# Values loaded row by row, and one weighting request per group that uses both column halves

## The chip, the cores and the metric

One core of a Trainium2 chip runs the kernel. The metric is device time in microseconds (us) of one execution. Engines: TensorE (PE; its weight loads are listed as PEld), VectorE (DVE), ScalarE (ACT), GpSimd (POOL) and SyncE (SP), whose queue issues all transfers (DMA) of this kernel. Matrix products read SBUF and write PSUM, which has 8 banks of 128 partitions x 512 32-bit columns.

## The reference

Eight batches of banded attention, and behind it a gated feed-forward block that mixes tokens:

```python
scores = scale * np.matmul(q, k.transpose(0, 1, 3, 2))      # 8 batches, 8 heads, 576 tokens, 64 wide
mask_plain = (rel >= 0) & (rel < window)                    # window 32: heads 0 to 3
mask_dil = (rel >= 0) & (rel < window * dilation) & (rel % dilation == 0)   # dilation 4: heads 4 to 7
attn = softmax(np.where(masks, scores, -1e9))
x = np.matmul(attn, v)                                      # heads side by side: 512 features a token
h = np.maximum(x @ w_in, 0.0)                               # 512 -> 1024
u, v = (h[..., :512], h[..., 512:])
v_n = (v - mean(v)) / np.sqrt(var(v) + 1e-06)
v_s = np.einsum('ts,bsd->btd', w_spatial, v_n) + b_spatial[None, :, None]
out = (u * v_s) @ w_out                                     # 512 -> 512
```

With a reordering of the dilated heads' tokens on the host, every head is a band: a block of 32 queries sees its own block of 32 keys and the one before.

## The kernel before, in words

**Tiling of the attention.** Heads are handled in pairs (hp, 4 a batch), two pairs make a group G (2 a batch, 16 in all). Within a group i is the pair, j the head in the pair. The 18 blocks of 32 queries are cut into 3 units of 6 blocks (`unit`, L776): the scores of a unit go to two banks (L796, stationary 64 x 32, moving 64 columns, rows 64j, columns 32(2i + j)), then the masks, the softmax (L830 to L861) and a transposition by VectorE (L866) that leaves the weights as `pT`, with the keys of (i, j) on partitions 32(2i + j).

**Values.** `values_in` (L763) loads a group's values into one buffer `kqv` of 11: four transfers, one for each (i, n), with n the block parity; the source is seen as "j k t d" (2 heads, 32 rows, 9 double blocks, 64 elements), the destination as 64 partitions x 9 x 64. A piece without a break is 64 elements of 4 bytes.

**Weighting.** `weighted` (L874) multiplies values by weights: for each half h of the tokens (9 blocks each) it asks for two banks, one per pair i, and for each key block c and each (i, j) issues one product with 32 rows (partitions 32(2i + j)), 64 stationary columns (the values) and 64 or 32 moving columns (the weights of one or two query blocks), L895. Its result goes to bank i, partitions 64j to 64j + 63: row group 2i + j always uses column half j. A half needs only the units that its blocks touch. After each half the weights whose blocks are over are given back, and four evacuations per group, `evacuated` (L918), copy the banks to `raw` on ScalarE (L927: 128 partitions x 288 columns, x64 in all).

**Behind the attention.** `features_in` (L931) splits `raw` into a high and a low part `x`; `v_tile` (L953, products L971 and L991) makes v and normalises it; `upper` (L1044), in the first batch, or `piece` (L1308, products L1279) makes u; `gate` (L1081, products L1091) mixes tokens; `piece` also makes the output in sums of block products, copied from the bank by ScalarE (L1365) or added by VectorE (L1342) and stored from `ur` (L1380). All 32-bit weights are split at the start into high and low parts, on ScalarE, VectorE, GpSimd or PE (`weight`, L565, with products L600 to L602; `spatial`, L633, with L651).

**What sets the order.** Nothing is scheduled by hand line by line. Each function above is a strand that yields what it waits for, the buffers it wants, and the engine with a planned cost. `Timeline.run` (L365) plays all strands against a model of the engines, always takes the one with the smallest planned start plus a share of its rank, and emits its instructions in that order into each engine's queue; on the chip each queue then runs in that order. The ranks are sums of a place in the batch and of numbers in the tables `SHIFT`, `SECOND`, `FIRST` and `RANKS`; `LOADS` (L239) is the order of the first loads on SP. `warm` (L1393) fills PE with products of zeros (L1399) while the planner's clock is under 30 us.

Of the kernel before, what the change touches and what calls it, by code (L numbers as in the profile page):

```python
# [26 lines left out]
    ('differences', 0): 3.431,  # L27
    ('differences', 1): -1.388,
    ('factor', 0): -1.117,
    ('factor', 1): 2.398,  # L30
    ('factor', 10): -3.001,
    ('factor', 11): 10.273,
    ('factor', 12): -3.976,
    ('factor', 13): 5.666,
    ('factor', 14): -7.301,
    ('factor', 2): 4.983,
    ('factor', 3): 0.711,
    ('factor', 4): 4.444,
    ('factor', 5): 2.348,
    ('factor', 6): 2.155,  # L40
    ('factor', 7): 1.428,
    ('factor', 8): 6.612,
    ('factor', 9): -2.995,
    ('features_in', 0): -0.537,
    ('features_in', 1): -0.751,
    ('features_in', 2): -1.809,
    ('features_in', 3): -0.424,
    ('gate', 0): -1.362,
    ('gate', 1): -1.076,
    ('gate', 2): -1.219,  # L50
    ('gate', 3): -2.27,
    ('gate', 4): -0.312,
    ('gate', 5): 0.11,
    ('gate', 6): -3.137,
    ('gate', 7): -0.085,
    ('heads_in', 0): -2.791,
    ('heads_in', 1): -12.584,
    ('heads_in', 2): -10.815,
    ('heads_in', 3): -13.398,
    ('piece', 0): -6.162,  # L60
    ('piece', 1): -3.011,
    ('piece', 10): 0.769,
    ('piece', 11): -5.597,
    ('piece', 12): -14.941,
    ('piece', 13): -3.803,
    ('piece', 14): 0.777,
    ('piece', 15): -2.117,
    ('piece', 16): 0.282,
    ('piece', 17): 1.018,
    ('piece', 18): -1.97,  # L70
    ('piece', 19): -1.676,
    ('piece', 2): -5.321,
    ('piece', 20): 1.502,
    ('piece', 21): 0.917,
    ('piece', 22): -2.788,
    ('piece', 23): 0.713,
    ('piece', 24): 1.033,
    ('piece', 25): -0.444,
    ('piece', 26): 1.61,
    ('piece', 27): 3.92,  # L80
    ('piece', 3): 0.345,
    ('piece', 4): -1.75,
    ('piece', 5): -7.219,
    ('piece', 6): -5.255,
    ('piece', 7): 0.574,
    ('piece', 8): -1.49,
    ('piece', 9): -6.48,
    ('unit', 0): 1.147,
    ('unit', 1): 0.659,
    ('unit', 2): 1.12,  # L90
    ('unit', 3): 1.555,
    ('unit', 4): 1.236,
    ('unit', 5): 0.864,
    ('v_tile', 0): -0.613,
    ('v_tile', 1): -2.171,
    ('v_tile', 2): 0.491,
    ('v_tile', 3): -0.547,
    ('v_tile', 4): 0.875,
    ('values_in', 0): 12.349,
    ('values_in', 1): 2.363,  # L100
    ('weighted', 0): 1.183,
    ('weighted', 1): -2.05,
}
SECOND = {
    ('differences', 0): 6.862,
    ('differences', 1): -4.682,
    ('factor', 0): -2.244,
    ('factor', 1): -7.324,
    ('factor', 10): -20.21,
    ('factor', 11): -11.603,  # L110
    ('factor', 12): -4.699,
    ('factor', 13): -10.917,
    ('factor', 14): 5.579,
    ('factor', 2): -2.131,
    ('factor', 3): -4.247,
    ('factor', 4): -1.839,
    ('factor', 5): 1.75,
    ('factor', 6): -3.017,
    ('factor', 7): 4.928,
    ('factor', 8): 6.82,  # L120
    ('factor', 9): -6.234,
    ('features_in', 0): -0.721,
    ('features_in', 1): 0.97,
    ('features_in', 2): -1.126,
    ('features_in', 3): 1.888,
    ('gate', 0): -4.65,
    ('gate', 1): -7.026,
    ('gate', 2): -9.988,
    ('gate', 3): -3.396,
    ('gate', 4): -7.372,  # L130
    ('gate', 5): -4.948,
    ('gate', 6): -4.213,
    ('gate', 7): -4.797,
    ('heads_in', 0): 2.901,
    ('heads_in', 1): 1.879,
    ('heads_in', 2): -11.28,
    ('heads_in', 3): -7.996,
    ('piece', 0): 6.664,
    ('piece', 1): -1.839,
    ('piece', 10): -3.696,  # L140
    ('piece', 11): -21.918,
    ('piece', 12): -4.586,
    ('piece', 13): 0.226,
    ('piece', 14): -13.768,
    ('piece', 15): -3.663,
    ('piece', 16): -5.818,
    ('piece', 17): -3.092,
    ('piece', 18): -3.654,
    ('piece', 19): 2.989,
    ('piece', 2): -6.168,  # L150
    ('piece', 20): -3.531,
    ('piece', 21): -29.215,
    ('piece', 22): -4.653,
    ('piece', 23): -2.368,
    ('piece', 24): -4.298,
    ('piece', 25): -7.047,
    ('piece', 26): 1.593,
    ('piece', 27): -8.907,
    ('piece', 3): -10.342,
    ('piece', 4): -9.305,  # L160
    ('piece', 5): 10.496,
    ('piece', 6): 3.592,
    ('piece', 7): 1.672,
    ('piece', 8): 2.058,
    ('piece', 9): -6.368,
    ('unit', 0): -4.01,
    ('unit', 1): -2.025,
    ('unit', 2): -3.272,
    ('unit', 3): -6.272,
    ('unit', 4): -8.821,  # L170
    ('unit', 5): -2.784,
    ('v_tile', 0): -5.232,
    ('v_tile', 1): -3.657,
    ('v_tile', 2): -2.764,
    ('v_tile', 3): -2.977,
    ('v_tile', 4): -3.818,
    ('values_in', 0): -10.326,
    ('values_in', 1): -3.974,
    ('weighted', 0): 1.018,
    ('weighted', 1): -10.872,  # L180
}
FIRST = {
    ('differences', 0): -17.708,
    ('factor', 0): -10.773,
    ('factor', 1): -8.285,
    ('factor', 10): -6.201,
    ('factor', 2): 9.259,
    ('factor', 3): -0.6,
    ('factor', 4): -12.498,
    ('factor', 5): -7.58,  # L190
    ('factor', 6): 5.807,
    ('factor', 7): -4.97,
    ('factor', 8): -9.831,
    ('factor', 9): -10.954,
    ('features_in', 0): -1.8,
    ('features_in', 1): -3.03,
    ('features_in', 2): 2.51,
    ('features_in', 3): 7.399,
    ('gate', 0): 6.142,
    ('gate', 1): 10.462,  # L200
    ('gate', 2): 2.373,
    ('gate', 3): -1.83,
    ('gate', 4): 1.615,
    ('gate', 5): 1.296,
    ('gate', 6): 1.467,
    ('gate', 7): 3.736,
    ('piece', 0): 0.034,
    ('piece', 1): -2.549,
    ('piece', 10): 0.916,
    ('piece', 11): -0.114,  # L210
    ('piece', 12): -6.838,
    ('piece', 13): 4.458,
    ('piece', 2): -2.984,
    ('piece', 3): 4.445,
    ('piece', 4): -18.587,
    ('piece', 5): -8.75,
    ('piece', 6): -2.472,
    ('piece', 7): -5.156,
    ('piece', 8): -0.366,
    ('piece', 9): -0.029,  # L220
    ('unit', 0): -16.896,
    ('unit', 1): -3.357,
    ('unit', 2): -3.181,
    ('unit', 3): -3.174,
    ('unit', 4): -3.978,
    ('unit', 5): -2.628,
    ('upper', 0): -2.081,
    ('upper', 1): -10.204,
    ('upper', 2): -0.74,
    ('upper', 3): 0.052,  # L230
    ('v_tile', 0): -2.1,
    ('v_tile', 1): -6.845,
    ('v_tile', 2): -1.186,
    ('v_tile', 3): -5.317,
# [172 lines left out]
def tile_banded_attention_gated_moe(  # L407
# [22 lines left out]
    nc = tc.nc  # L430

    B, NPAIR, _, S = kT.shape
# [1149 lines left out]
```

## Time and profile before

| | |
|---|---|
| time, median of 3 runs | 601.1 us (600.82 to 604.26) |
| the profiled execution's own time | 601.41 us |
| its span, first to last instruction | 599.6 us |
| busy | PE 540.0, DVE 381.1, ACT 334.3, POOL 191.8 us |
[...]

The span is cut into stretches below. [...] A busy time can only be read beside the waits: an engine that is idle while another is the bound costs nothing.

### The profile page before, as it was taken

Reading aid. Unit: us, or ns where it says so; the run is one execution under the profiler, and the core shown is the slowest. Engines: PE = TensorE matmul, PEld = TensorE weight load, DVE = VectorE, ACT = ScalarE, POOL = GpSimd, SP = SyncE. Lnnn points to the kernel's source line nnn. Section 1 sums busy time; section 2 is a strip of 40 time slices with the busy share of each in tenths; the row PEclk is TensorE's granted clock in tenths of the full one; section 3 lists DMA queues with packets and bytes.
Section 4 is the critical chain, followed back from the end, with each engine's and each line's share of the span. In section 5 each row is a group of like instructions: output and inputs, shape, how many; then the busy total and the mean of one; then the engine's idle time right before and its main releaser. Section 6 shows DMA issues by size and latency. Waiting matters only on the chain.

```text
span 599.6 us, 18457 instructions
## 1 busy us (share of the span) xinstructions
PE 540.0 (90%) x7828; PEld 492.3 (82%) x7828; DVE 381.1 (64%) x878; ACT 334.3 (56%) x938; POOL 191.8 (32%) x226
## 2 busy tenths in 40 slices
PE   9803898689989996999999999999998999999997
PEld 6603676689889975988999889898998899899997
DVE  6611687659995483766686567745784578647545
ACT  5711679454775453664576367454874478447414
POOL 4300015413841442222441264225431363226100
PEclk9965899879999997999999999999999999999999
DMA  8322713133242212222014221232114302100102
GB/s 295 126 67 77 256 35 109 40 108 97 52 139 59 58 45 86 59 57 88 21 47 113 56 89 59 78 97 90 52 37 133 102 21 59 45 1 21 61 2 79
DMA packets 58535, 46.71 MB, mean 78 GB/s; under 512 B 39378, under 2 KB 48594, under 8 KB 58452
## 3 DMA queue, kind: packets, MB, share of 16 engines
q1 hardware_dynamic: 58452, 45.53, 25.4%
q8 instruction: 61, 1.00, 0.7%
q14 instruction: 22, 0.18, 0.1%
HBM read 36.08 MB, written 9.44 MB: 76 GB/s over the span
## 4 chain that ended last, share of the span: by engine, by line
PE 72%; DMA 9%; DVE 8%; SPq 4%; issue 3%; ACT 2%; POOL 1%; DVEq 0%; ACTq 0%; POOLq 0%
PE bank L1279 26%; PE bank L1091 15%; PE bank L971 12%; PE bank L895 6%; PE bank L796 5%; DMA kqv<-in_vw_dram 4%; DMA out_dram<-ur 3%; SPq L771 2%; DMA kqv<-in_qT_dram 2%; PE bank L991 2%; PE bank L1399 2%; PE bank L1071 1%; PE bank L1070 1%; DVE fac L537 1%; PE bank L600 1%
## 5 line engine op out<-in xcount | busy, mean ns | idle before, releaser
L1091 PE MATMUL bank<-wt,fac 128*128 128x288 f32 x768 | 115.7, 300 | 0.8 <-ACT ur L1365 0.8
L1091 PEld LDWEIGHTS bank<-wt,fac 128*128 128x128 f32 x768 | 106.9, 190 | 2.8 <-ACT ur L1365 1.3
L971 PE MATMUL bank<-wih,x 128*128 128x512 f32 x256 | 84.6, 397 | 0.0
L895 PE MATMUL bank<-pT,kqv 32*64 32x64 f32 (+1 forms) x2688 | 49.2, 226 | 38.4 <-DMA kqv<-in_vw_dram 30.4
L1365 ACT COPY ur<-bank 128x288 f32<-128x288 f32 x120 | 47.0, 397 | 59.5 <-PE bank L1279 33.6
L895 PEld LDWEIGHTS bank<-pT,kqv 32*64 32x64 f32 x2688 | 46.3, 140 | 39.8 <-DMA kqv<-in_vw_dram 31.5
L838 ACT ACTIVATE p<-p,nm 128x64 f32<-128x64 f32 x180 | 60.4, 342 | 10.7 <-DVE nm L832 10.7
L861 POOL TENSOR_TENSOR p<-p,rv 128x384 f32<-128x384 f32 x48 | 41.0, 855 | 71.1 <-DVE rv L859 71.1
L1016 POOL TENSOR_TENSOR rs<-rs,halfneg 128x1 f32<-128x1 f32 (+1 forms) x40 | 30.4, 761 | 100.1 <-DVE rs L1013 99.5
L1279 PE MATMUL bank<-fac,woh 128*128 128x288 f32 x256 | 55.0, 305 | 6.9 <-ACT ur L1365 5.8
L971 PEld LDWEIGHTS bank<-wih,x 128*128 128x128 f32 x256 | 49.4, 193 | 10.2
L537 DVE TENSOR_TENSOR x<-raw,x 128x576 fp32r<-128x576 f32 x32 | 29.8, 933 | 38.2 <-ACT x L942 38.2
L927 ACT COPY raw<-bank 128x288 f32<-128x288 f32 x64 | 30.5, 561 | 41.8 <-PE bank L895 41.4
L1342 DVE TENSOR_TENSOR ur<-ur,bank 128x288 f32<-128x288 f32 x90 | 39.3, 448 | 20.5 <-PE bank L1279 14.8
L1208 ACT CAST fac<-ur 128x576 fp32r<-128x576 f32 x56 | 36.8, 670 | 26.1 <-DVE ur L1077 22.4
L971 PE MATMUL bank<-wil,x 128*128 128x512 f32 x128 | 50.8, 397 | 0.0
L537 DVE TENSOR_TENSOR fac<-ur,fac 128x576 fp32r<-128x576 f32 x56 | 42.4, 779 | 12.6 <-ACT fac L1208 12.4
L1265 POOL TENSOR_TENSOR ur<-ur,ur 128x576 f32<-128x576 f32 x28 | 41.4, 1481 | 26.9 <-DVE fac L537 19.7
L1279 PEld LDWEIGHTS bank<-fac,woh 128*128 128x128 f32 x256 | 42.4, 193 | 9.2 <-ACT ur L1365 6.3
L866 DVE STREAM_TRANSPOSE pT<-p 128x384 f32<-128x384 f32 x48 | 27.2, 571 | 33.7 <-PE bank L895 25.0
L796 PE MATMUL bank<-kqv 64*32 64x64 f32 x2304 | 41.4, 219 | 6.6 <-issue 3.4
L1265 POOL TENSOR_TENSOR raw<-raw,raw 128x576 f32<-128x576 f32 x21 | 30.2, 1437 | 50.8 <-DVE fac L537 26.7
(157 smaller groups left out, 1159.9 us busy)
## 6 DMA issues: line engine op xcount, KB each, us to landing
kqv<-in_vw_dram SPq DMA_DIRECT2D x64, 144.0 KB
out_dram<-ur SPq DMA_DIRECT2D x64, 144.0 KB
kqv<-in_kT_dram SPq DMA_DIRECT2D x30, 288.0 KB
kqv<-in_qT_dram SPq DMA_DIRECT2D x30, 288.0 KB
kqv<-in_w_in_dram SPq DMA_DIRECT2D x8, 512.0 KB
kqv<-in_w_out_dram SPq DMA_DIRECT2D x4, 512.0 KB
kqv<-in_w_spT_dram SPq DMA_DIRECT2D x5, 288.0 KB
kqv<-in_kT_dram SPq DMA_DIRECT2D x2, 192.0 KB
```

The costliest lines, as they stand in the source:

```text
L537: nc.vector.tensor_sub(out, a, b.bitcast(F32))
L796: nc.tensor.matmul(s[w][q * QB : q * QB + QB, e, :], kq[r, :S].rearrange("p (u n i t) -> p u t n i", n=2, i=QB, t=US)[:, (u + places[b, pa ...
L838: nc.scalar.activation(p[:, e, j], s[j][:, e] if first else p[:, e, j], AF.Exp, bias=nm[:, i : i + 1], scale=SCALE if first else 1.0, accu ...
L861: nc.gpsimd.tensor_mul(flat, flat, spread_out(rv))
L895: nc.tensor.matmul(acc[i][1][1][j * D : j * D + D, o : o + len(run) * QB], v[r, c * D : c * D + D], probs[b, G, u][1][r, at : at + len(run ...
L971: nc.tensor.matmul(pm, x[a][:, cols], wi[w][:, c, NF:], start=c == 0 and n == 0, stop=c == NC - 1 and n == 2)
L1091: nc.tensor.matmul(pv, left[:, a, i, m * P : m * P + P], wt[:, k, h, w, i], start=n == 0, stop=False, skip_group_check=True)
L1208: nc.scalar.copy(dst[:, 0], src)
L1265: (eng.tensor_add if kind == "s" and n == 1 else eng.tensor_sub)(at(to), at(left), at(right))
L1279: nc.tensor.matmul(bank[:, :HS], lhs, rhs, start=fresh and n == 0, stop=n == 5, skip_group_check=not fresh or kind == "s")
L1342: nc.vector.tensor_add(ob[1][:, m], ob[1][:, m], bank[:, :HS])
L1365: nc.scalar.copy(ob[1][:, m], bank[:, :HS])
```

## The change

Four things change, and the tables of ranks and the order of loads with them.

- `values_in` issues eight transfers per group in place of four, one for each (i, n, j), each with 32 rows outermost in source and destination; the planned cost goes from 2.6 + 1.5 to 4.2 + 2.0.
- `weighted` asks once per group: for all three units' weights and the values, four banks and `raw`. Its products are the same 84 per group, in an order in which one key block's products of token half 0 and of token half 1 take turns; those of half 1 write column half 1 - j in place of j. Weights and values are given back at the end. The planned cost is 1.35 in place of 0.8 twice.
- `evacuated` waits for the whole group; for token half 1 it copies twice 64 partitions, crosswise, in place of once 128.
- planned costs of `unit` (0.6 to 0.68, the first group's 0.72 to 0.77) and of the transposition (0.47 to 0.5) change, which emit the same instructions.

```diff
 SHIFT = {
-    ('differences', 0): 3.431,
+    ('differences', 0): 0.468,
...
 LOADS = """
-wi00 wi10 kq1a kq0a kq1b kq0b kq3 sp0 kq2 sp3 wi12 sp1 bias wo2 wi11 v1 wi01 v0 sp2 wi02 wo0 wi03 wo3 wi13 wo1
-sp4
+sp4 kq1b wi00 wi12 kq0a kq0b kq1a kq2 wi11 kq3 wi10 wo0 v0 v1 sp3 wi03 wi02 sp2 sp1 wi13 wi01 wo3 wo1 sp0 wo2
+bias
 """.split()
...
-        (big,) = yield DMA, 2.6, 1.5
+        (big,) = yield DMA, 4.2, 2.0
         for i, n in itertools.product(range(2), range(2)):
             src = vw[b, 2 * G + i, (n + 1) * QB : (n + 2) * QB].rearrange("k (t j d) -> j k t d", j=2, d=D)
-            dst = big[1][:, :BIG].rearrange("p (t n d) -> p t n d", n=2, d=D)
-            nc.sync.dma_start(dst[i * 2 * QB : (i + 1) * 2 * QB, :, n, :], src)
+            for j in range(2):
+                to = (2 * i + j) * QB
+                nc.sync.dma_start(big[1][to : to + QB, :BIG].rearrange("p (t n d) -> p t n d", n=2, d=D)[:, :, n, :], src[j])
...
+        yield [("pT", b, G, u) for u in range(NU)] + [("values", b, G)]
+        yield "av bank av bank av bank av bank raw"
+        got = yield PE, 1.35, 0.0
+        acc = [[got[4 * h + 2 * i : 4 * h + 2 * i + 2] for i in range(2)] for h in range(2)]
...
+        runs = []
         for h in range(2):
+            for c in range(h * HB - h, h * HB + HB):
+                to = [g for g in (c, c + 1) if h * HB <= g < h * HB + HB]
+                split = len({g // (2 * US) for g in to}) > 1
+                runs += [(len([r for r in runs if r[1] == h]) + n, h, c, run) for n, run in enumerate([[g] for g in to] if split else [to])]
+        for n, h, c, run in sorted(runs):
...
+            for i, j in itertools.product(range(2), range(2)):
                 r = slice((2 * i + j) * QB, (2 * i + j + 1) * QB)
+                col = (j ^ h) * D
+                nc.tensor.matmul(
+                    acc[h][i][1][1][col : col + D, o : o + len(run) * QB],
...
-        yield ACT, 0.465 if hp >= NPAIR // 2 else 0.3, 0.1
-        nc.scalar.copy(dst, acc[1][1][:, :HS].rearrange("p (r j) -> p r j", r=2))
+        src = acc[1][1][:, :HS].rearrange("p (r j) -> p r j", r=2)
+        for n in range(1 + h):
+            yield ACT, 0.465 if hp >= NPAIR // 2 else 0.3, 0.1
+            to, at = (slice(n * D, n * D + D), slice(D - n * D, 2 * D - n * D)) if h else (slice(0, P), slice(0, P))
+            nc.scalar.copy(dst[to], src[at])
```

## Rows read from the trace of the kernel before

**Rows 1.** Busy time by stretch; after PEclk the DMA share and GB/s.

```profile
0.00:27.00 27.00, 24.18 (x371) 18.42 (x372) 17.60 (x55) 16.99 (x62) 10.61 (x24) 1.00 0.68 230
27.00:55.00 28.00, 3.90 (x29) 2.67 (x31) 3.87 (x10) 3.18 (x9) 2.23 (x3) 0.64 0.27 72
55.00:66.00 11.00, 10.13 (x335) 8.86 (x336) 6.88 (x14) 7.78 (x16) 0.00 (x0) 0.82 0.61 206
66.00:130.00 64.00, 53.54 (x821) 44.28 (x820) 40.88 (x97) 39.83 (x113) 19.76 (x24) 0.89 0.32 94
130.00:250.00 120.00, 110.58 (x1453) 100.85 (x1449) 86.44 (x198) 68.68 (x191) 48.88 (x53) 0.97 0.25 71
250.00:566.00 316.00, 307.36 (x4627) 287.35 (x4619) 207.90 (x476) 188.29 (x530) 110.31 (x124) 1.00 0.22 64
```

**Rows 2.** Who waited for whom: PE to 66, 66 to 130, 200 to 320; ACT.

```profile
PE bank L895 <- DMA kqv<-in_vw_dram: 24.1, 3, 12.1
...
PE bank L895 <- DMA kqv<-in_vw_dram: 6.3, 2, 4.6
...
PE bank L1279 <- ACT ur L1365: 5.8, 1, 5.8
...
ACT ur L1365 <- DMA out_dram<-ur: 6.4, 1, 6.4
```

**Rows 3.** SP's queue: issues by line (ns least/median/most), then in order of time.

```profile
L771 SPq DMA_DIRECT2D kqv<-in_vw_dram x64: 537/3980/7048, 14.2 to 505.0; - x64
...
L753 SPq DMA_DIRECT2D kqv<-in_kT_dram x34: 328/432/4118, 1.6 to 473.3; - x34
...
14.22 15.85 SPq L771 DMA_DIRECT2D kqv<-in_vw_dram  x4
...
34.20 13.92 SPq L771 DMA_DIRECT2D kqv<-in_vw_dram  x4
...
217.96 4.15 SPq L771 DMA_DIRECT2D kqv<-in_vw_dram  x1
...
226.82 18.92 SPq L1380 DMA_DIRECT2D out_dram<-ur  x6
```

**Rows 4.** Busy time of a stretch in which values alone are loaded, columns as before.

```profile
500.00:508.00 8.00, 8.00 (x145) 7.70 (x145) 7.14 (x18) 5.86 (x18) 2.49 (x3) 1.00 0.16 37
```

**Rows 5.** Issues by size (queries as keys; the spatial blocks are 288 KB too).

```profile
kqv<-in_kT_dram SPq DMA_DIRECT2D x30, 288.0 KB
...
kqv<-in_w_in_dram SPq DMA_DIRECT2D x8, 512.0 KB
```

**Rows 6.** The weighting on PE: a group in order of time; a stretch, L895 alone.

```profile
384.04 2.75 PE L895 MATMUL bank<-pT,kqv 32*64 32x64 f32 x168
...
54.85:59.10 4.25, 4.25 (x156) 4.24 (x156) 0.53 0.17 67
```

**Rows 7.** The scores on PE in order of time.

```profile
95.55 0.89 PE L796 MATMUL bank<-kqv 64*32 64x64 f32 x48
...
106.67 1.56 PE L796 MATMUL bank<-kqv 64*32 64x64 f32 x96
```

**Rows 8.** From the chain: a 32-bit product of 288 columns, two instructions.

```profile
79.58 0.48 PE bank L651 x2
```

**Rows 9.** A stop inside the weighting; instructions of PE; the instruction queue.

```profile
262.88 0.42 PE L895 MATMUL bank<-pT,kqv 32*64 32x64 f32 x11 [0.94 <-issue]
...
PE 540.0 (90%) x7828; PEld 492.3 (82%) x7828; DVE 381.1 (64%) x878; ACT 334.3 (56%) x938; POOL 191.8 (32%) x226
...
q8 instruction: 61, 1.00, 0.7%
```

**Rows 10.** ScalarE's copies by line: 1 partition, 128 partitions, and the evacuation.

```profile
L713 ACT CAST wb<-kqv x2: 667/667/667, 17.7 to 18.4; 1x576 fp32r<-1x576 f32 x2
...
L657 ACT CAST wa<-kqv x1: 677/677/677, 76.7 to 76.7; 128x576 fp32r<-128x576 f32 x1
...
L927 ACT COPY raw<-bank 128x288 f32<-128x288 f32 x64 | 30.5, 561 | 41.8 <-PE bank L895 41.4
```

More of the change, by code (lines that the diff above doesn't have):

```diff
@@ new lines @@
+    ('piece', 27): 2.135,
+    ('piece', 3): -2.111,
+    ('piece', 4): -2.378,
+    ('piece', 5): 1.404,
+    ('piece', 6): -1.667,
+    ('piece', 7): -0.342,
+    ('piece', 8): -2.98,
+    ('piece', 9): -6.786,
+    ('unit', 0): 0.628,
+    ('unit', 1): 0.566,
+    ('unit', 2): 1.826,
+    ('unit', 3): 0.588,
+    ('unit', 4): 0.52,
+    ('unit', 5): 0.142,
+    ('v_tile', 0): -0.502,
+    ('v_tile', 1): 0.902,
+    ('v_tile', 2): -0.127,
+    ('v_tile', 3): -1.002,
+    ('v_tile', 4): -0.803,
@@ new lines @@
+    ('piece', 20): -11.571,
+    ('piece', 21): -1.952,
+    ('piece', 22): -17.589,
+    ('piece', 23): -4.77,
+    ('piece', 24): -8.189,
+    ('piece', 25): -13.354,
+    ('piece', 26): -12.138,
+    ('piece', 27): -7.139,
+    ('piece', 3): -3.759,
+    ('piece', 4): 2.184,
+    ('piece', 5): -10.825,
+    ('piece', 6): -2.88,
+    ('piece', 7): 0.609,
+    ('piece', 8): 2.008,
+    ('piece', 9): 1.439,
+    ('unit', 0): -2.064,
+    ('unit', 1): -1.584,
+    ('unit', 2): -2.985,
+    ('unit', 3): 1.179,
@@ new lines @@
+    ('factor', 6): -2.949,
+    ('factor', 7): -1.43,
+    ('factor', 8): -1.637,
+    ('factor', 9): 1.108,
+    ('features_in', 0): 2.028,
+    ('features_in', 1): -0.853,
+    ('features_in', 2): -4.587,
+    ('features_in', 3): 2.266,
+    ('gate', 0): -3.573,
+    ('gate', 1): -2.15,
+    ('gate', 2): -1.355,
+    ('gate', 3): -12.755,
+    ('gate', 4): 1.063,
+    ('gate', 5): -0.7,
+    ('gate', 6): -6.356,
+    ('gate', 7): 5.24,
+    ('piece', 0): -3.587,
+    ('piece', 1): 0.61,
+    ('piece', 10): 1.419,
@@ new lines @@
+    ('piece', 11): -4.959,
+    ('piece', 12): -7.293,
+    ('piece', 13): 5.036,
+    ('piece', 2): -5.483,
+    ('piece', 3): -0.264,
+    ('piece', 4): 0.068,
+    ('piece', 5): -0.742,
+    ('piece', 6): -6.641,
+    ('piece', 7): -15.959,
+    ('piece', 8): 1.594,
+    ('piece', 9): 1.925,
+    ('unit', 0): -5.725,
+    ('unit', 1): -4.044,
+    ('unit', 2): -5.345,
+    ('unit', 3): -0.772,
+    ('unit', 4): -2.004,
+    ('unit', 5): 0.239,
+    ('upper', 0): -9.059,
+    ('upper', 1): 0.37,
@@ L913, in tile_banded_attention_gated_moe @@
+        tl.done("weighted", b, G)
+        for u in range(NU):
+            tl.give(probs[b, G, u])
+        tl.give(values[b, G])
+        for h, i in itertools.product(range(2), range(2)):
+            products[b, 2 * G + i, h] = acc[h][i]
     raws = {}
```

436 lines of the change are left out of this document (169 added, 267 removed).

## The prediction

> **What bounds the kernel now.** I read the busy times by stage first [rows 1]. From 250 to 566 us TensorE (PE) is busy 307.4 of 316 us at the full clock: there it is the bound, and only work taken off PE shortens that stretch. The start is different. From 27 to 55 us PE is busy 3.9 of 28 us, VectorE 3.9 and ScalarE 3.2: nobody works. From 66 to 130 PE is busy 53.5 of 64 at a mean clock of 0.89, from 130 to 250 it is busy 110.6 of 120. The waits of PE say why [rows 2]: 24.1 us until 66 and 6.3 us until 130 are the weighting (L895) waiting for transfers of values; 5.8 us between 200 and 320 is a product waiting for ScalarE's copy L1365, which itself waited 6.4 us for an output transfer to free its buffer. The queue of SyncE (SP) shows why those are late [rows 3]. The four transfers of one group's values hold SP for 15.85 and 13.92 us (median 3.98 us each over all 64), where the median transfer of keys holds it 0.43 us. The second set starts at 34.20, after the first and a weight block stuck behind it, and the weighting that wants it runs from 54.85 [rows 6]. At 217.96 the last of such a set is again in the way: the keys behind it go at 222, the output transfers only at 226.82. While values alone move, 0.16 of the 16 transfer engines are busy and 37 GB/s flow [rows 4], that is two engines or a little more; the first 27 us of the kernel moved 230 GB/s at 0.68 [rows 1].
>
> **Values with rows outermost.** Before, a transfer's source had the two heads as its outermost dimension, 2; after, eight transfers per group have 32 rows outermost on both sides. If a transfer is dealt out by its outermost dimension, 2 explains the two engines, and 32 lets all 16 work: 16/2 x 37 = 296 GB/s, so a group's 590 KB (4 x 144 KB) take 2.0 us. On SP 8 issues cost 8 x 0.43 = 3.4 us, or 8 x 0.54 = 4.3 by the shortest issue of a values transfer [rows 3], in place of some 14 to 16 us. Bounds: at best the waits vanish; at worst it is 8 x 2 us with the same two engines, as now. [...] Here 34 transfers of keys hold SP 0.43 us each in the median, so whatever a transfer costs beyond that overlaps with the next [rows 3].
>
> What that is worth, by stage. The idle stretch: the first weighting starts at 54.85; all it needs except values is there by 27. In the new order of loads two groups' values (1.2 MB) stand behind five weight blocks of 512 KB, one of 288 and four pairs of keys and queries of 576 KB [rows 5], 5.3 MB; 6.5 MB at 230 GB/s [rows 1] is 28 us, the first group's 26. The weighting starts near 28: **27 us** off (bounds 0, if another wait stands there, and 28). What is late next is the rest of the weights: the loads bring 10.5 MB by 66 us (27 x 230, 28 x 72, 11 x 206 [rows 1]), which at 230 GB/s is 46 us; that is the bound of the second rival. Second batch: 6.3 us of waits go, and PE comes out of them at half clock; I take **8 us** (bounds 0 and 10.5, all of PE's idle time from 66 to 130). The output transfer behind values: **5 us** of 5.8 (bounds 0 and 9.4, all idle time from 130 to 250).
>
> **The weighting.** A group is 84 products of 32 bits, which PE runs as 168 instructions in 2.75 us at full clock [rows 6]. With four (row group, column half) tiles each row group uses one half of the columns. [...] A second row says that two tiles in the same rows and different columns do run together: the scores (L796) have four tiles, two in each half of the rows, and 96 take 1.56, 48 take 0.89, so (1.56 - 0.89)/48 = 14 ns each [rows 7]. An instruction of a 32-bit product streams 288 columns in 0.48/2 = 0.24 us [rows 8], so 64 in 53 ns: over four tiles 13.3. Had tiles in the same rows shut each other out it would be 27. So in the change, where the halves of tokens h = 0 and 1 take turns on opposite columns, eight tiles run: the part that streams, 2.75 - (0.89 - 0.67) = 2.53, halves to 1.27, with 0.22 of entry 1.49 us: 1.26 off per group. The ends: 0 (weight loads of one row group may share a path, which no row shows), 1.38 (half of all), and below nothing the drain of the third rival; I take 1.26, as the row of the scores is the nearest.
>
> Part of it comes back. In the middle of dense small products PE stops for 0.9 to 1.0 us with nothing to wait for, three times, of which one row stands here [rows 9]. An instruction queue brings 1.00 MB in 61 packets, and PE has 2 x 7828 instructions, about 257 to a packet [rows 9]; so I take it that a stop comes when a packet's worth is eaten faster than the next arrives. Twice as fast means longer stops and more of them: I charge 0.3 us a group. Net 0.96 x 16 = **15 us**.
>
> One request in place of two: it wants four banks at once, but before both halves already ran without a break (168 in one piece), so nothing new is held. It waits for all three units' transposed weights where h = 0 waited for two; those of a batch are ready long before in the steady stretch. Behind it on PE the next products would wait; I cost this at nothing, covered by the products between scores and weighting, and at 1 us a group if the cover is gone. `evacuated` for h = 0 starts when the group is done: 1.49 us after its start, some 0.1 us later than now (half of 2.75).
>
> **Evacuation.** For h = 1 two copies of 64 partitions: 32 more on ScalarE. A copy with 1 partition costs 667 ns, one with 128 costs 677 [rows 10], so half the partitions save nothing: at the copy's mean of 0.56 [rows 10] 32 are 18 us of ScalarE, 2.2 a batch, where it is busy 188 of 316 us. Hidden, except in the first batch, where features wait for it: **+1 us** (bounds 0 and 4 x 0.56 in each of two batches, 4.5).
>
> **New plan.** The ranks only reorder. With PE busy 307.4 of 316 it can bring at most 8.6 us there; if it left PE as loose as from 130 to 250 (92%) it would cost 16. I take 0. Moved loads: the last spatial block goes from last to first on SP, the bias rows from the thirteenth place to the end, the values from sixteenth and eighteenth to thirteenth and fourteenth; each load still holds SP some 0.43 us for the same bytes.
>
> **Sum.** The profiled execution took 601.4 us (span 599.6 and 1.8 around it; the runs' median is 601.1). 601.4 - 27 - 8 - 5 - 15 + 1 = **547.4 us**.
>
> **Rivals.**
> 1. *Eight tiles are no faster than four*, because weight loads of one row group share a path, or because 15 to 16 ns is what an instruction costs. For: 64 and 32 columns wide products together take 2.53 us, where streaming alone (28 x 53 + 14 x 27 ns per tile) is 1.87. [...] Then 547.4 + 15 = 562.4. [...]
> 2. *The start is bound by the other loads.* 10.5 MB at 206 to 230 GB/s need 46 to 51 us and were in by 66: the last weight comes 15 to 20 us sooner, and if all waits for it and half a group's work is lost besides, 35 us of gain shrink to 12. 547.4 + 23 = 570.4. Against: the products after the first weighting need one load at a time, and from 55 to 66 PE was busy 10.1 of 11 while loads still came.
> 3. *Slower: changing the column half drains the array.* Each group alternates 20 times between h = 0 and 1; at the 0.22 us of a burst's entry (0.89 - 0.67 [rows 7]) that is 4.4 us a group, 70 in all: 562.4 + 70 = 632.4. It decides from 39/(16 x 20) = 0.12 us a change, where the 39 us of the other parts are gone. Against: the scores alternate column tiles at every product, in 14 ns.
> 4. *Transfers don't spread*: two engines as before. Then only the weighting and the copies count: 601.4 - 15 + 1 = 587.4.
>
> **How the numbers follow.** Forecast 0.60, rival 1 0.17, rival 2 0.14, rival 4 0.05, rival 3 0.04. The likeliest's own range is 532 to 560. The range asked for reaches down by PE's other idle time (8.6 from 250 to 566, 4.4 of the 9.4 before) and up past rivals 1 and 2: 528 to 575, leaving out 3 and 4 and a tail. About 1% is what a measurement of this kernel tells from no change. All cases but rival 3 are faster by over 2%; I keep 0.04 for a mixture near nothing: faster 0.92, same 0.04, slower 0.04.
>
> **What would show it.** SP's issues of values near 0.4 to 0.5 us each, eight per group, and a far higher GB/s while they move; no long wait of PE for values; the first weighting before 32 us; 168 weighting products in 1.4 to 1.6 us (2.7 says rival 1) with stops of about 1 to 2 us in more groups; 96 copies at L927's successor, 32 of them on 64 partitions at no less than 0.38 us; batches about 2 us shorter. I am wrong if a values issue still takes 2 us or more, if PE idles over 10 us in one piece after 10 us, or if batches don't shorten.

## The result and the profile after

The median is 550.2 us after (548.4 to 551.9, four runs) against 602.5 before on the same chip: ratio 0.913, interval 0.909 to 0.918. The profiled execution took 551.9 us, span 550.2. Times of runs below are medians; that of shift152 leaves out the longest of its six runs, which lies over 1.5% above its kernel's fastest. The forecast was 547.4 in a range of 528 to 575. So the total came out, and the question for the runs is whether its terms did.

Busy time by stretch, of after (columns as in [rows 1]: from:to and length in us; busy us of PE, PEld, DVE, ACT and POOL, with the number of instructions in brackets; the granted clock of PE as a share of its full clock; the busy share of the core's 16 transfer engines; the GB/s that they moved):

```profile
0.00:27.00 27.00, 25.65 (x474) 19.14 (x474) 19.81 (x58) 15.73 (x58) 9.67 (x23) 1.00 0.80 235
27.00:55.00 28.00, 24.69 (x306) 17.63 (x307) 15.01 (x31) 21.91 (x47) 3.13 (x4) 0.94 0.67 226
55.00:66.00 11.00, 11.00 (x179) 8.06 (x178) 10.52 (x28) 10.62 (x30) 1.62 (x5) 1.00 0.56 159
66.00:130.00 64.00, 58.61 (x979) 52.33 (x977) 57.23 (x133) 44.45 (x133) 36.70 (x40) 0.99 0.25 67
130.00:250.00 120.00, 117.01 (x1840) 108.11 (x1841) 84.92 (x195) 81.21 (x228) 44.44 (x51) 0.98 0.31 86
250.00:520.00 270.00, 264.53 (x3870) 247.18 (x3870) 183.34 (x410) 177.42 (x460) 98.68 (x107) 0.99 0.21 61
```

The dead stretch of 27 to 55 us is gone: PE is busy 24.7 of 28 us where it was 3.9 [rows 1], and the transfers run on at 226 GB/s where they fell to 72. SP's queue says by what. Its issues of values by line (ns least/median/most):

```profile
L772 SPq DMA_DIRECT2D kqv<-in_vw_dram x128: 560/608/1777, 11.5 to 419.1; - x128
```

and in order of time, two groups in one go and the next one:

```profile
11.45 16.07 SPq L772 DMA_DIRECT2D kqv<-in_vw_dram  x16
53.09 5.52 SPq L772 DMA_DIRECT2D kqv<-in_vw_dram  x8
```

A transfer of half the size holds SP for 608 ns in the median instead of 3980, so a group costs SP 5.5 to 8 us instead of some 14 to 16 [rows 3]. Who waits for whom, PE, of after:

```profile
PE bank L897 <- issue: 7.2, 4, 2.1
PE bank L1281 <- ACT ur L1367: 6.0, 1, 6.0
PE bank L1281 <- ACT raw L929: 1.5, 1, 1.5
PE bank L1093 <- ACT x L944: 1.1, 1, 1.1
```

No wait for values is left (30.4 us in [rows 2]). Two kinds stay. One is stops at L897, the weighting, in which PE waits for nothing the profile shows ("issue"). The 1.5 us put down to the copy L929 and the 1.1 us put down to the cast L944 are counted with them: they stand at the same count of instructions, and PE goes on as long after the landing of a packet of its instruction queue as at the others (experiment 5). The copy had ended 0.4 us before; the cast ends just as PE goes on, so that it had a part isn't excluded. The other kind is one wait of 6.0 us for ScalarE's copy L1367. It has the look of the 5.8 us in [rows 2], but isn't the same: there ScalarE waited for an output transfer, here nothing waits for a transfer; the copy is the end of a chain (ScalarE's waits there are 2.2 us for GpSimd's L1267 and 1.9 for VectorE's L537).

The weighting in order of time, first a group with no stop, then one with a stop; and from the page the lines of its copies and its products:

```profile
282.53 2.02 PE L897 MATMUL bank<-pT,kqv 32*64 32x64 f32 x168
...
458.10 2.03 PE L897 MATMUL bank<-pT,kqv 32*64 32x64 f32 x167
...
461.91 0.18 PE L897 MATMUL bank<-pT,kqv 32*64 32x32 f32 x1 [1.78 <-issue]
```

```profile
L929 ACT COPY raw<-bank 64x288 f32<-64x288 f32 (+1 forms) x96 | 49.7, 541 | 16.0 <-PE bank L897 14.7
...
L897 PE MATMUL bank<-pT,kqv 32*64 32x64 f32 (+1 forms) x2688 | 34.8, 229 | 8.0 <-issue 7.2
```

168 instructions take 2.02 us where [rows 6] has 2.75: 0.73 us off a group, not the 1.26 forecast. That is the best case: of the twelve groups that run in one piece five take 2.02 and the others 2.1 to 2.5 us, for a reason that no run shows. In the second group 167 of them run, PE stops for 1.78 us, and the last one follows. The copies behave as forecast: 96, mean 541 ns, the half ones hardly cheaper (538 ns against 548; [rows 10]: 561).

### The profile page after: what moved, and what is told of

Its sections match the earlier page's. It is cut to its first block, busy times and chain, and to the rows that moved or that the text cites. A ratio compares the mean times of both kernels' runs of the same rounds, so it can differ in the third digit from the quotient of the medians.

```text
span 550.2 us, 18561 instructions
## 1 busy us (share of the span) xinstructions
PE 527.7 (96%) x7836; PEld 478.2 (87%) x7836; DVE 385.4 (70%) x878; ACT 360.1 (65%) x970; POOL 194.2 (35%) x226
## 4 chain that ended last, share of the span: by engine, by line
PE 76%; DVE 9%; ACT 6%; DMA 5%; issue 2%; SPq 1%; POOL 0%; DVEq 0%; ACTq 0%
PE bank L1281 31%; PE bank L1093 16%; PE bank L973 12%; PE bank L897 6%; PE bank L797 4%; PE bank L993 2%; DMA kqv<-in_w_in_dram 2%; DMA kqv<-in_w_out_dram 2%; ACT raw L929 2%; PE bank L1073 1%; PE bank L1072 1%; SPq L772 1%; DMA kqv<-in_kT_dram 1%; PE bank L1060 1%; DVE x L537 1%
## 5 line engine op out<-in xcount | busy, mean ns | idle before, releaser
L862 POOL TENSOR_TENSOR p<-p,rv 128x384 f32<-128x384 f32 x48 | 42.6, 888 | 123.6 <-DVE rv L860 122.0
L839 ACT ACTIVATE p<-p,nm 128x64 f32<-128x64 f32 x180 | 60.4, 337 | 10.9 <-DVE nm L833 10.8
L1367 ACT COPY ur<-bank 128x288 f32<-128x288 f32 x120 | 45.7, 397 | 32.4 <-PE bank L1281 28.9
L929 ACT COPY raw<-bank 64x288 f32<-64x288 f32 (+1 forms) x96 | 49.7, 541 | 16.0 <-PE bank L897 14.7
L537 DVE TENSOR_TENSOR fac<-ur,fac 128x576 fp32r<-128x576 f32 x56 | 47.3, 859 | 10.2 <-ACT fac L1210 10.2
L1281 PE MATMUL bank<-fac,woh 128*128 128x288 f32 x256 | 54.1, 302 | 0.0
L1018 POOL TENSOR_TENSOR rs<-rs,halfneg 128x1 f32<-128x1 f32 (+1 forms) x40 | 28.4, 710 | 68.5 <-DVE rs L1015 68.2
L1267 POOL TENSOR_TENSOR raw<-raw,raw 128x576 f32<-128x576 f32 x21 | 33.8, 1608 | 51.6 <-DVE fac L537 40.1
L1210 ACT CAST fac<-ur 128x576 fp32r<-128x576 f32 x56 | 36.7, 673 | 22.9 <-POOL ur L1267 12.5
L1281 PE MATMUL bank<-fac,o 128*128 128x288 f32 x288 | 44.7, 302 | 6.2 <-ACT ur L1367 6.0
L1344 DVE TENSOR_TENSOR ur<-ur,bank 128x288 f32<-128x288 f32 x90 | 39.2, 448 | 14.6 <-PE bank L1281 10.0
L1281 PEld LDWEIGHTS bank<-fac,o 128*128 128x128 f32 x288 | 41.3, 194 | 7.3 <-ACT ur L1367 6.5
L1267 POOL TENSOR_TENSOR ur<-ur,ur 128x576 f32<-128x576 f32 x28 | 41.3, 1475 | 11.8 <-DVE fac L537 8.1
L1281 PEld LDWEIGHTS bank<-fac,woh 128*128 128x128 f32 x256 | 42.8, 193 | 1.9
L897 PE MATMUL bank<-pT,kqv 32*64 32x64 f32 (+1 forms) x2688 | 34.8, 229 | 8.0 <-issue 7.2
L797 PEld LDWEIGHTS bank<-kqv 64*32 64x32 f32 x2304 | 34.8, 119 | 7.3 <-issue 5.9
L897 PEld LDWEIGHTS bank<-pT,kqv 32*64 32x64 f32 x2688 | 32.1, 130 | 10.2 <-issue 8.9
```

Of the source, the lines that this page charges most:

```text
L537: nc.vector.tensor_sub(out, a, b.bitcast(F32))
L797: nc.tensor.matmul(s[w][q * QB : q * QB + QB, e, :], kq[r, :S].rearrange("p (u n i t) -> p u t n i", n=2, i=QB, t=US)[:, (u + places[b, pa ...
L839: nc.scalar.activation(p[:, e, j], s[j][:, e] if first else p[:, e, j], AF.Exp, bias=nm[:, i : i + 1], scale=SCALE if first else 1.0, accu ...
L862: nc.gpsimd.tensor_mul(flat, flat, spread_out(rv))
L897: nc.tensor.matmul(acc[h][i][1][1][col : col + D, o : o + len(run) * QB], v[r, c * D : c * D + D], probs[b, G, u][1][r, at : at + len(run) ...
L929: nc.scalar.copy(dst[to], src[at])
```

## The experiments

Twelve kernels. All ratios are against the kernel before, run beside them on the same chip.

**1. The transfers alone (rows_only), and the rest alone (no_rows).** The first is the kernel before with this edit and nothing else, the second the changed kernel with it undone:

```diff
-            dst = big[1][:, :BIG].rearrange("p (t n d) -> p t n d", n=2, d=D)
-            nc.sync.dma_start(dst[i * 2 * QB : (i + 1) * 2 * QB, :, n, :], src)
+            for j in range(2):
+                to = (2 * i + j) * QB
+                nc.sync.dma_start(big[1][to : to + QB, :BIG].rearrange("p (t n d) -> p t n d", n=2, d=D)[:, :, n, :], src[j])
```

> The kernel before, plan and order kept, with its four transfers of a group's values replaced by the eight with 32 rows outermost. If the transfers' shape is what gave the larger part (theory): about 602.5 - 40 = 562 us, SP's issue of a group's values 5 to 6 us in place of 13 to 16, no wait of TensorE for values over 2 us. If the gain needs the new plan, whose planned costs fit the faster transfers (rival): 585 us or more, with new waits in the place of the old.

> The kernel after, plan and order kept, with the four transfers of before. Theory: the 40 us come back, about 590 us, waits for values of 20 us or more in the first 130 us. Rival (the new order of loads alone, values ahead of weights, would have done it): 565 us or less.

rows_only: 551.3 us, ratio 0.916 (0.912 to 0.920). The eight transfers alone bring 51.5 us, all of the change's gain within the error, where the forecast gave them 40. no_rows: 576.6 us, ratio 0.958 (0.954 to 0.961). Taking them out of the changed kernel costs 26.4 us, only half as much. Matched product by product, no_rows falls 23 us behind the changed kernel in the first 60 us, about as far as the kernel before falls behind rows_only there, and 6.6 more between 160 and 200 us; at the other places where the kernel before loses time (below) it loses none. What in the new order of work spares them was not taken apart. Busy time of two stretches and one wait, of rows_only:

```profile
27.00:55.00 28.00, 23.93 (x398) 18.33 (x397) 18.85 (x39) 18.65 (x41) 1.78 (x2) 0.94 0.62 193
...
66.00:130.00 64.00, 62.28 (x1029) 55.60 (x1026) 56.05 (x135) 46.61 (x149) 36.25 (x38) 1.00 0.33 79
```

```profile
PE bank L896 <- DMA kqv<-in_vw_dram: 1.4, 2, 1.2
```

and of no_rows, the first stretch, PE's longest waits and ScalarE's for transfers:

```profile
27.00:55.00 28.00, 11.64 (x190) 9.04 (x190) 4.32 (x11) 5.38 (x21) 3.43 (x4) 0.65 0.29 80
```

```profile
PE bank L601 <- ACT woh L624: 9.7, 1, 9.7
PE bank L896 <- DMA kqv<-in_vw_dram: 8.7, 2, 5.2
...
ACT kqv L585 <- DMA kqv<-in_w_in_dram: 21.4, 5, 13.8
...
ACT ur L1366 <- DMA out_dram<-ur: 5.1, 1, 5.1
```

SP's queue in no_rows, in order of time:

```profile
12.55 33.40 SPq L771 DMA_DIRECT2D kqv<-in_vw_dram  x8
46.06 3.91 SPq L630 DMA_DIRECT2D kqv<-in_w_spT_dram  x1
50.08 0.84 SPq L562 DMA_DIRECT2D kqv<-in_w_in_dram  x2
```

Eight old transfers hold SP for 33.4 us, and the blocks of weights behind them go out after 46 us. ScalarE waits 13.8 us for one of those (L585), and PE 9.7 us for the copy L624 that ScalarE makes behind it. The old transfers hold up the loads, whoever stands behind them; the 5.1 us, which end at 163 us, are for an output transfer behind values.

Laid on the trace of before by the count of each line's products, rows_only is ahead by 23.7 us at 59 us, 36.2 at 127, 44.8 at 265 and 51.2 at 528. So the first stretch gave 24 (forecast 27), the second batch 12.5 (8), what follows to 265 us 8.6 (5), and the rest 6.4 (0).

Two things make up the excess. One is the clock: up to PE's last product the trace of before has 44.4 us at half clock (0.50), that of rows_only 3.4. PE is busy in 19.0 us of the one and all of the other, and half of the difference, 7.8 us, I count as lost work: an estimate from the products of L1281 in the changed kernel, of which 12 in a row take 3.25 us at a granted clock of 0.50 (from 131.58 us) and 1.75 at 1.00 (from 139.08). Nearly all of it lies in or behind the three places where PE had waited: 35 to 59 us, 117 to 127 and 229.5 to 236. The other is that output transfers stood behind values in four more batches. Of the kernel before, ScalarE's waits for them from 250 to 566 us, PE's waits from 265 to 528 us, and one of the four places in order of time:

```profile
ACT ur L1365 <- DMA out_dram<-ur: 18.9, 4, 5.0
...
PE bank L895 <- issue: 4.2, 4, 1.4
PE bank L796 <- issue: 1.9, 2, 1.0
PE bank L1091 <- ACT ur L1365: 0.8, 2, 0.4
...
333.42 0.58 DVE L866 STREAM_TRANSPOSE pT<-p 128x384 f32<-128x384 f32 x1 [1.38 <-POOL p L861]
...
334.10 2.11 PE L895 MATMUL bank<-pT,kqv 32*64 32x64 f32 x119 [1.45 <-issue]
```

After its wait ScalarE makes the exponentials late, so VectorE transposes the weights late, and PE begins the weighting 0.1 us after the transposition ends, at all four places; the profile names no releaser there, but these are waits and not the stops of experiment 5, whose count of instructions they don't share. rows_only has neither ScalarE's waits nor these of PE; its two stops in the same work come to 2.0 us, where before has 1.9 (L796). Its lead grows at just these places, by 2.3 us at 334, 1.0 at 397 and 2.4 at 460. Added up, rows_only waits 29.0 us less for values, 6.6 less for the copies L1365 and 2.5 less for queries, none of the 4.2 us for late weights, and loses 7.8 less to the clock: 50.1 of the 51.5 us.

**2. Where the weighting's gain comes from (two_copies, h_outer).** In two_copies both token halves use the same column half; the copies stay 96. In h_outer the opposite halves stay, but the first token half is done before the second begins:

```diff
 two_copies
-                col = (j ^ h) * D
+                col = j * D
...
-            to, at = (slice(n * D, n * D + D), slice(D - n * D, 2 * D - n * D)) if h else (slice(0, P), slice(0, P))
+            to, at = (slice(n * D, n * D + D), slice(n * D, n * D + D)) if h else (slice(0, P), slice(0, P))
 h_outer
-        for n, h, c, run in sorted(runs):
+        for n, h, c, run in sorted(runs, key=lambda x: (x[1], x[0])):
```

> The kernel after with token half 1 in the same column half as token half 0 (four tiles in place of eight); the two copies of 64 partitions stay, straight in place of crosswise, every instruction at its place. Theory: the stream of a group's 168 instructions goes back from 1.80 to about 2.53 us, 16 x 0.73 = 12 us, less some 3 us of shorter stops for instructions: 558 to 562 us. Rival (TensorE's time for the weighting is hidden by other waits): 551 us or less, with 2.5 us a group all the same.

> The kernel after with all products of token half 0 before those of half 1, opposite column halves kept: the turns alone are undone. Theory (TensorE starts products in their order, so only products near each other overlap): about 2.5 us a group as with four tiles, 558 to 562 us. Rival (what counts is only that the other column half is free, TensorE reaches ahead): 1.8 us a group, 550 us.

two_copies: 556.5 us, 0.924 (0.920 to 0.927). h_outer: 551.9 us, 0.917 (0.914 to 0.921). A group of each in order of time, two_copies first:

```profile
340.27 2.65 PE L897 MATMUL bank<-pT,kqv 32*64 32x64 f32 x168
```

```profile
336.41 2.55 PE L897 MATMUL bank<-pT,kqv 32*64 32x64 f32 x168
```

2.65 us with four tiles in use, 2.55 with all eight but one column half of a row group after the other, 2.02 with all eight in turn, 2.75 in the order of before. So it is the eight tiles in turn that shorten a group, and changing the column half at every turn costs nothing that shows in 2.02: the third rival is out. In time, straight halves cost 6.3 us against the changed kernel (16 x 0.63 = 10 in the groups), which is more than the error of about 3.6; the turns alone, 1.7 us, are within it.

**3. The copies (one_copy).** As two_copies, with the two half copies of a run joined:

```diff
-            nc.scalar.copy(dst[to], src[at])
+            if h and n == 0:
+                continue
+            nc.scalar.copy(dst, src)
```

> two_copies (556.5 us), with the 64 half copies of a run joined again into 32 of 128 partitions, as the kernel before has them; the products, their order and the plan as in two_copies. ScalarE does 32 copies of about 0.53 us less, some 17 us of its busy time. Theory: ScalarE (65% busy) is not what the products wait for, so the extra copies are covered: within 1.5 us of 556.5. Rival: the copies delay the exponentials and the ScalarE copies of the last step, on which TensorE waits: 552 us or less.

553.5 us, 0.919 (0.916 to 0.922): 3.0 us less than two_copies, between the two theories and about the size of the error. Its 64 copies keep ScalarE busy 338.8 us where two_copies has 358.9; 20 us of work off ScalarE are worth at most a few on the end.

**4. The tables (old_plan, new_tables).** The planner's shifts, ranks and order of loads exchanged: old_plan is the changed kernel with the tables of before, new_tables is rows_only with those of after.

```diff
 SHIFT = {
...
-    ('weighted', 0): -3.76,
-    ('weighted', 1): -3.947,
+    ('weighted', 0): 1.183,
+    ('weighted', 1): -2.05,
...
```

> The changed code with the tables of the kernel before (shifts, ranks, order of loads). Theory: the new tables bring nothing of their own in the steady stretch; they cut the products into 18 requests in two batches where the old ones have 8, which costs 47.2 against 45.9 us. With the old tables the values transfers start where rows_only had them, so the start is as good as rows_only's (551.3 us) and the faster weighting (0.73 us a group, 11.7 in 16 groups) comes on top, less about 5 us of stops and copies: 543 to 550 us, products in two batches at 45.9 to 46.2 us. Rival: the new tables are needed, since the old ones were found for a weighting that is twice as many requests and for copies of 128 partitions: 553 us or more.

> rows_only (551.3 us), with the tables of the changed kernel in place of its own; nothing else differs. Theory: a table of shifts only holds the work together for the program it was made for; old_plan lost some 61 us with the wrong one, by dozens of gaps of 1 to 5 us and the low clock behind them, so this one loses tens of us as well: 570 to 620 us. Rival: the new tables are better tables, whatever they plan (that would explain why the changed kernel with the old ones is so slow): 545 to 553 us.

old_plan: 611.1 us, ratio 1.016 (1.012 to 1.019). new_tables: 607.2 us, ratio 1.013 (1.006 to 1.020). My theory for old_plan was wrong by over 60 us, the rival right, though it gave no size beyond 553 us or more; with that seen, the theory for new_tables held. PE's longest waits, of old_plan and of new_tables:

```profile
PE bank L1281 <- DVE fac L537: 13.8, 7, 3.7
PE bank L897 <- issue: 8.0, 5, 2.6
PE bank L797 <- DMA kqv<-in_qT_dram: 7.8, 3, 4.8
PE bank L973 <- ACT x L944: 6.1, 2, 4.7
```

```profile
PE bank L1280 <- ACT fac L1209: 20.8, 3, 8.1
PE bank L896 <- issue: 9.6, 7, 2.1
```

No single wait explains it: gaps of 1 to 8 us at many lines, and behind them 65 us at half clock in old_plan and 55 in new_tables, against 13.7 in the changed kernel and 3.4 in rows_only. Neither set is the better one. Each holds the order together for its own code, and on the other's code it loses 56 to 61 us.

**5. The stops (shift104, shift152, fewer8, fewer12).** The stops stand where PE's instructions, weight loads and those of its sequencer included, have counted to 193 more than a multiple of 256: seven in after with 11.6 us in all, five in before with 8.3, six in rows_only with 7.9. A stop is counted from the start of the last instruction before that place to the start of the next, so that some 0.2 us of each is still that instruction's own time.

What PE waits for stands in the traces too: the landing of each of the packets of its instruction queue, 16 KB each [rows 9]. At all 109 stops of over 0.25 us in the fourteen traces PE goes on 1.2 to 1.8 us (median 1.4) after the landing of the packet whose number is that of the boundary; for the six longest of after 1.3 to 1.5. At the boundaries that it crosses without a stop, that packet had landed at least 1.1 us before. At no crossing had more than one packet beyond it landed. So I take the stops as waits for code.

To move them and nothing else, some products of zeros at the start (`warm`) are split in two or left out:

```diff
 shift104: 52 products in halves (shift152: 76)
-            nc.tensor.matmul(got[0][1].rearrange("p (n c) -> p n c", n=4), z, z.unsqueeze(1).broadcast_to([P, 4, P]), start=True, stop=True)
+            to = got[0][1].rearrange("p (n c) -> p n c", n=4)
+            for n in [2, 2] if k < 52 else [4]:
+                nc.tensor.matmul(to[:, :n], z, z.unsqueeze(1).broadcast_to([P, n, P]), start=True, stop=True)
+            k += 1
 fewer8: 8 left out (fewer12: 12, range(30, 78, 4))
+            if k not in range(30, 78, 6):
```

> The changed kernel; 52 of the products of zeros at the start are made in two of 256 columns, so that every later instruction of TensorE stands 104 places further on; nothing else changes. Theory: TensorE stops where it crosses from one block of 256 instructions into the next less than about 3.4 us after the last crossing, because the next block of code is not there yet; moved by 104 places, laid over the recorded starts of the changed kernel, the crossings give stops of 9.7 us in all where the places of now give 12.8 (recorded: 11.6), and the stops at 336, 346 and 460 us of the changed kernel go or move elsewhere: 546 to 549 us. Rival: the stops belong to the weighting (banks, the change of column halves) and not to the count of instructions: the same stops at the same groups, 549.5 to 551.5 us.

> As shift104, with 76 products of zeros in halves, so 152 places. Theory: the crossings fall into the weighting groups more often: 16.9 us of stops, 4 more than at the places of now, 7 more than in shift104: 553 to 556 us. Rival: the same stops at the same groups, 549.5 to 551.5 us, and no difference from shift104.

shift104: 558.4 us, 0.924 (0.921 to 0.928). shift152: 564.1 us, 0.937 (0.933 to 0.941). The stops moved as the count says. Laid over the changed kernel's starts with 3.5 us for a block, a shift of 152 puts stops of about 1.6 us and more at 27, 76, 153, 164, 277, 288, 402, 413 and 476 us; the trace has one of 1.1 to 2.9 us at each of these places (at 31 to 486 us, as its time has grown), and the changed kernel's own near 337 and 461 are gone. Between the two runs lie 5.7 us, near the 7 expected. But they are 8 and 14 us slower than the changed kernel where I had said -3 and +4. The sum of the stops (14.6 and 18.8 us) covers 3.0 and 7.2 of that. The rest lies behind the stops. The same work in shift104 (in order of time, then the stretch behind the stop):

```profile
99.22 1.66 PE L897 MATMUL bank<-pT,kqv 32*64 32x64 f32 x136 [0.63 <-DVE pT L867]
103.06 0.86 PE L897 MATMUL bank<-pT,kqv 32*64 32x64 f32 x32 [2.18 <-issue]
```

```profile
103.20:106.20 3.00, 3.00 (x42) 2.94 (x43) 0.00 (x0) 2.51 (x4) 0.00 (x0) 0.50 0.37 92
```

and in the changed kernel, where the boundary doesn't fall into this group:

```profile
95.34 2.02 PE L897 MATMUL bank<-pT,kqv 32*64 32x64 f32 x168 [0.63 <-DVE pT L867]
```

After the stop of 2.18 us the granted clock is 0.50, at which 12 products of L1281 took 3.25 us instead of 1.75 (experiment 1). At half clock shift104 spends 23.9 us and shift152 27.3, against 13.7; PE is busy in 21.9 and 23.9 us of it, against 10.9, and half of the difference, 5.5 and 6.5 us, is lost work by the same estimate. 3.0 + 5.5 = 8.5 and 7.2 + 6.5 = 13.7; measured 8.2 and 13.9 (the two profiled executions themselves 6.4 and 15.1). So by that estimate a stop of 2 us cost up to two and a half times itself: in shift104 one of 2.16 us that ends at 79.84 is followed by 6.1 us of products at half clock. Not every one did: behind a stop of 2.15 us that ends at 348.55 in the changed kernel the clock stayed at 1.00.

> The changed kernel without 8 of its 78 products of zeros, taken out one in six after the first 30, so that what follows stands 16 of TensorE's instructions further forward. shift104 and shift152 moved the stops as the count said, but were 8 and 15 us slower where I had expected -3 and +4: about half of a long stop's price comes after it, at the low clock, and both had three more stretches of it. Theory: by the count (3.3 to 3.6 us from one crossing to the next), the crossings at 337, 347 and 460 us lose 1 us or more of their stops each, two of 0.8 to 1.6 come in near 152 and 276, and the half-speed stretch behind 460 us goes (1.7 us): 545.5 to 549 us. Rival: the sum of the stops doesn't fall (more of them short), or the missing zeros cost clock at the start: 550 to 554 us.

> As fewer8, 12 products of zeros less, 24 instructions. Theory: the crossings near 337 and 460 us lose their stops altogether, the one near 152 grows to 2 us, near 276 and 287 one of 1.3 and one of 0.6 us appear: in sum as fewer8, 545.5 to 550 us, with the half-speed stretch, if any, behind 152 us and none behind 460. Rival: 550 to 554 us, stops where the changed kernel has them.

fewer8: 549.9 us, 0.914 (0.910 to 0.918). fewer12: 549.5 us, 0.913 (0.910 to 0.917). No gain beyond the error: the first lies between its two ranges, the second in that of its theory. The stops again stand at the count, but not all where I had put them: fewer8 has none near 152 and 276 us and one of 1.7 us at 200, fewer12 none near 276 and 287 and one of 1.5 us at 202. In the group that had been cut after 167 products, fewer12 has no stop, and full clock behind it:

```profile
457.82 2.05 PE L897 MATMUL bank<-pT,kqv 32*64 32x64 f32 x168
```

```profile
463.40:466.60 3.20, 3.20 (x26) 3.09 (x24) 1.66 (x4) 3.08 (x12) 0.34 (x1) 1.00 0.00 0
```

The changed kernel in the same stretch, and in the one behind its wait of 6.0 us:

```profile
463.40:466.60 3.20, 3.20 (x15) 3.20 (x14) 0.95 (x2) 2.01 (x5) 0.00 (x0) 0.50 0.00 0
...
129.00:135.50 6.50, 3.92 (x16) 3.92 (x17) 4.74 (x8) 3.48 (x9) 1.48 (x1) 0.50 0.27 77
```

In exchange fewer12 has a new stop of 1.95 us at 155 and 6.8 us at half clock from 27: the stops sum to 9.5 us instead of 11.6, the low clock to as much as before.

**6. More instructions in a row (twice).** Each group's products made twice, with nothing between:

```diff
-        for n, h, c, run in sorted(runs):
+        for n, h, c, run in sorted(runs) * 2:
```

> The changed kernel with the products of each weighting group made twice in a row (the second time over the same sums, begun anew); everything else is as it was. The 168 further instructions of a group (336 with their weight loads) stream in 1.80 us at the pace of the first. Theory: TensorE's code comes in blocks of 256 instructions, one in 3.0 to 4.3 us by the stops of the runs so far; so 672 instructions in one go need two or three blocks and the second pass costs, beside 1.80 us, two stops of about 2 us in most groups, some of them with a stretch at half clock behind: 16 x 4 to 6 us = 64 to 96 us, 614 to 646 us. Rival: the stops belong to what stands around the weighting, and the second pass costs what it streams: 16 x 1.80 = 29 us, 579 us, at most 585.

643.8 us, ratio 1.071 (1.065 to 1.077): 93.6 us more than the changed kernel, 5.8 a group, where streaming alone would be 29 in all. PE's longest wait, and a group in order of time:

```profile
PE bank L897 <- issue: 44.0, 23, 3.5
```

```profile
324.09 2.21 PE L897 MATMUL bank<-pT,kqv 32*64 32x32 f32 x128 [2.14 <-issue]
328.09 0.86 PE L897 MATMUL bank<-pT,kqv 32*64 32x64 f32 x30 [1.79 <-issue]
```

Between two stops run 128 products, and with their 128 weight loads that is a block of 256 instructions; from stop to stop 328.09 - 324.09 = 4.0 us pass. So in one go PE got no more than 128 products per 3.1 to 4.3 us (over most stops of all these runs), where a group without a stop took 168 in 2.02 us. A crossing took up to 3.6 us (two_copies). The theory's 614 to 646 us held, the rival's 579 to 585 fell.

## Why the prediction was right, and which of its terms were not

- **Transfers, 27 + 8 + 5 = 40 us: measured 51.5** (rows_only). What the prediction wanted to see held: eight issues with 32 rows outermost, SP free after 5.5 to 8 us, 1.4 us of waits for values left. That the outermost dimension deals a transfer out was an assumption, and no run counts the engines; what shows is that with 2 outermost 0.16 of the 16 engines were busy and 37 GB/s flowed while values alone moved [rows 4], and with 32 outermost 0.52 and 118 GB/s (after, 417 to 420.5 us). The 296 GB/s and 2.0 us a group of the prediction no run shows: eight transfers of 72 KB, issued one per 0.61 us, come to some 120 GB/s. The smaller size did no harm that shows (2.6 us from issue to landing, median of the 128 in after). The sizes were off: 24 us for the idle stretch (27), 12.5 for the second batch (8), 8.6 for the output transfer (5), and 6.4 later, for which I had nothing. Two steps failed. "I take 8 us" and its like price a wait at its own length, and the low clock that follows a wait was added to none but the second batch. And "The output transfer behind values" was priced at one place, where four later batches had the same wait on ScalarE: there rows_only gained the 6.4 us.
- **Second rival** (bound by the other loads): from 27 to 55 us the transfers run at 226 GB/s and PE is busy 24.7 us. The loads were not the bound. The fourth (transfers don't spread) falls with the same numbers, the third (draining) with 2.02 us a group. Of the first this much is true, that eight tiles (2.02 us a group) are not twice as fast as four (2.65 in two_copies).
- **Weighting, 1.26 us gross and 0.96 net a group, 15 us: the step that failed.** No run shows the 1.26: gross it is 0.73 (2.75 to 2.02), 11.7 us in 16 groups, in the best of them. That "the part that streams" halves is wrong: 2.53 us became 1.80 (2.02 - 0.22), 10.8 ns an instruction and not 7.6. Eight tiles in turn are faster than four (2.02 against 2.65 in two_copies), but not twice as fast. At a granted clock of 0.53 one took 27 ns (156 in 4.25 us) and at the full clock 16 [rows 6], so a fixed price of an instruction, the first rival's other reason, does not explain it alone; what holds the 10.8 ns is open. Two of the eight tiles share each row group, and whether their weight loads hold each other up no run takes apart. In the steady stretch two batches take 124.9 us against 126.7 before and 123.2 in rows_only, so batches are 0.9 us shorter and not the 2 forecast, and the gain of the weighting is eaten there by stops (4.5 us in these two batches).
- **Stops, 0.3 us a group, 4.8 us**: 11.6 us of stops in after against 8.3 in before and 7.9 in rows_only, so 3.3 to 3.7 more; by where the count falls the sum lies between 8.9 (fewer8) and 18.8 (shift152). The prediction read three stops in before; two more, of 1.5 and 2.9 us, stand at 18.5 and 68 us. "A stop comes when a packet's worth is eaten faster than the next arrives" is what twice, the four shifted kernels and the landings of the packets show. What was missing is their price in clock, by the estimate of experiment 1 half of PE's busy time at the granted clock of 0.50 behind them.
- **Copies, +1**: 3.0 us between two_copies and one_copy, within the bounds of 0 and 4.5 and hardly more than the error. The two rows that it rested on were casts of 576 columns and not copies; the copies show the same (538 ns with 64 partitions, 548 with 128).
- **New plan, 0**: against rows_only the changed kernel has the one wait of 6.0 us, in every run with its transfers, its weighting and its tables (4.5 to 6.0), and PE is busy 10.9 us at half clock where it was 3.4, so by that estimate 3.7 lost. The weighting's 11.7 less 3.7 of stops less 6.0 less 3.7 is -1.7; rows_only in turn has 1.4 us of waits for values that the changed kernel lacks. Within a few us they cancel, and the ratios say the same: 0.913 against 0.916, with intervals that overlap by most of their width. "The ranks only reorder" was right only for a table on its own code; the cross-overs cost 56 to 61 us, so as a part of this change the new tables were not free to leave out.

So the total of 547.4 was near 550.2 by luck: 11.5 us too little on the transfers and 13 too much on the rest (14 forecast, 1 found) nearly cancel. No version here beats both kernels by more than the error: rows_only, fewer8, fewer12 and the changed kernel lie within 2 us of each other.

## What to carry to other kernels

Price a wait of PE by what follows it as well: read the granted clock of the stretch behind it, and where it is 0.50, add half of PE's busy time in it (here 12 products took 3.25 us there instead of 1.75). And look for the same wait in every later batch, on the engines that feed PE too: here ScalarE's waits (18.9 us in four batches of before) came back in part as PE's. Before making dense small products faster, count their instructions: over most stops of these runs a block of 256 took 3.1 to 4.3 us, and the faster groups here gave part of their gain back (11.6 us of stops against 8.3). And where the order of work comes from a fitted table, an edit and its table are one change; test an edit whose plan stays the same (here the eight transfers) alone, first.

## What the runs showed of the hardware that I had not expected

- The transfers with 2 outermost did not only move 37 GB/s; each held the issuing queue for about 4 us (median 3.98 of 64), so all that stood behind them was late too. Of the smaller ones with 32 outermost each held it for 0.61 us in the median of 128.
- In these traces TensorE's code comes at a rate: in packets of 256 instructions (61 for the 15743 of after), never more than one block ahead, and at the stops PE went on 1.4 us after one landed (median of 109). In twice its blocks set the pace: 44.0 us of PE's time are stops, and 85 us of the span are at half clock.
- Leaving out a dozen products of zeros, or splitting them, moved stops and low clock hundreds of microseconds later; the four such kernels and the changed one, which differ in nothing else, lie between 549.5 and 564.1 us. A difference of 1 to 2% between two versions of such a kernel can be this and nothing else.
